# Loads of queries, keys and values cut into pieces of some 1.3 KB with gaps between them in DRAM, for all but the first four units

## The chip, the cores and the metric

The kernel runs on one core of a Trainium2 chip. The metric is the device time of one execution in microseconds (us). TensorE is PE in the rows, its weight loads PEld; VectorE is DVE, ScalarE ACT, GpSimd POOL, and SyncE is SP. SP issues the loads, ACT the stores. All of them go through the same 16 DMA engines of the core. The rows call the queue of SP's transfers q1, that of ACT's q10, and those that bring instructions q8 and q14.

## What is computed

Attention for 8 batches and 8 heads with 32 global and 512 local positions (head size 64): a global position looks at all positions, a local one at the 32 global ones and at the local ones at most 32 away. On its output `x` (8 x 576 x 512) a gated layer follows:

```
s_g = scale * q_g @ k_all^T                 out_g = softmax(s_g) @ v_all
s_l = concat(scale * q_l @ k_g^T, where(|i-j| <= 32, scale * q_l @ k_l^T, -1e9))
out_l = softmax(s_l) @ concat(v_g, v_l)
x = heads side by side (8 x 576 x 512)
gate = sigmoid(sum over k of conv_w[k] * x[position - 4 + k])       (5 taps)
result = (gate * (x @ w_val)) @ w_out
```

## The kernel before

The host lays the inputs out anew (`_layout`, ahead of the launch and outside the time). Two heads of one batch make a unit, so there are 32 units (`NU`), four to a batch. For each unit there is one array of queries and keys, 128 partitions x 1248 floats (`qk`, 4992 bytes a row), and one of values, 128 x 1950 floats (`vw`, 7800 bytes a row: 15 windows x 2 heads x 65).

Each unit is loaded by two transfers, `load_qk(u)` and `load_v(u)`, which go through `transfer` (`nc.sync.dma_start`) into one of 4 buffers for each kind. A row of the array is one contiguous stretch in DRAM and one in the partition it goes to. The weights come in 8 more transfers; those of `w_val` are cut into four stretches of 1 KB a partition, those of `w_out` come as rows of 4 KB. Thirteen loads are issued first of all (`FIRST`: the mask, q/k and v of units 0 to 3, the four parts of `w_val`); every later load has a place in one long line that is written out by hand (`ORDER`: `iq5` issues the q/k load of unit 5, `iv5` its v load, `wi4` the load of a weight). `transfer` ties a later load to the last PE instruction ahead of it in that line, so that a load is issued when PE has come that far.

The same line fixes the order of all work on each engine. For unit u: `s` are 128 small score matmuls on q/k (`l_s`, L522), `mx` and `exp` the softmax on DVE and ACT, `t` the transposes (L555, or L263 in halves of 64 rows), `av` 128 small matmuls on v (`l_av`, L574), `eps`/`norm` the division, `xt` a transpose (L601), `conv` the taps of the gate on DVE. For batch b: `gs`, `gav` are the scores and the weighted sums of the global positions (L425 and L477, the latter needs v of all four units), `g1`/`g2` the large matmuls of the gated layer (L706, L734), `ob` the copy of a result into one of 3 buffers and `st` its store of 256 KB, issued by ACT. From about 280 us on no unit is left and PE runs g1 and g2 almost alone.

Of the kernel before, what the change touches and what calls it, by code (L numbers as in the profile page):

```python
# [19 lines left out]
B, H, SL, SG, D = 8, 8, 512, 32, 64  # L20
DM = H * D
KW = 5
P = 128
NDT = DM // P
NU = B * NDT
NC32 = SL // 32
NPOS = 21
NWIN = 14
SCALE = 0.125
NEG = -1.0e30  # L30
QC = SL + 2 * SG
QK = QC + NPOS * 32


def chunk_pos(c):
    return c + c // 3


def win_pos(w):
    return w + w // 3  # L40


def block_win(m):
    return min(max(m - 1, 0), NWIN - 1)


def pos_chunk(p):
    return -1 if p % 4 == 3 else p - p // 4
# [113 lines left out]
FIRST = "q0 m0 q1 w0 q2 v0 q3 w1 v1 w2 v2 w3 v3"  # L162
# [78 lines left out]
def attention_moe(ctx, tc, qk, vw, maskd, w_val, w_out, out):  # L241
# [27 lines left out]
    small = cp.tile([P, 2 * P + NDT * KW * 2], I32, name="small")  # L269
    mask = small[:, :2 * P].bitcast(mybir.dt.bfloat16).rearrange("p (i c) -> p i c", i=4)  # L270
# [75 lines left out]
    def transfer(out, in_):  # L346


        ins = nc.sync.dma_start(out, in_).ins
        if last_pe:  # L350
            tc.add_manual_dep(ins, last_pe[0].name, after, reason="a load's place in the line")
# [43 lines left out]

    loads = {}

    def load_qk(u):
        t = sb.tile([P, QK], F32, tag="qk", name=f"qk{u}", bufs=RINGS["qk"])
        transfer(t, qk[u])  # L400
        loads.setdefault(u, [None, None])[0] = t

    def load_v(u):
        t = sb.tile([P, NWIN + 1, 2, E1], F32, tag="v", name=f"v{u}", bufs=RINGS["v"])
        transfer(t, vw[u])
        loads.setdefault(u, [None, None])[1] = t


# [3 lines left out]
    def g_s(b):  # L412
        units = [loads[u][0] for u in range(NDT * b, NDT * b + NDT)]
        s = [pair(f"gs{b}.{h}").rearrange("p a c -> p (a c)")[:, P:P + 544] for h in range(2)]
        for part in range(2):
            for n in range(8):
# [5 lines left out]
                else:  # L422
                    keys = qkt[rows, QC + 512:QK]
                cols = slice(0, 384) if part == 0 else slice(384, 544)
# [398 lines left out]
    for u in range(NU):  # L823
        if ("qk", u) not in first:
            plan.add(f"iq{u}", "SP", lambda u=u: load_qk(u), [f"iq{u - 1}"] if ("qk", u - 1) not in first else [],
                     take=[("qk", u)])
            plan.add(f"lq{u}", "DMA", lambda: None, [f"iq{u}"])
        if ("v", u) not in first:
            plan.add(f"iv{u}", "SP", lambda u=u: load_v(u), [f"iq{u}"] if ("qk", u) not in first else [],
                     take=[("v", u)])  # L830
            plan.add(f"lv{u}", "DMA", lambda: None, [f"iv{u}"])

    for b in range(B):
# [3 lines left out]
        for h in range(2):  # L837
            n = f"{b}.{h}"
# [111 lines left out]
    with tc.manual_schedule():  # L950
        for kind_, n in first:
            if kind_ == "qk":
                load_qk(n)
            elif kind_ == "v":
                load_v(n)
            elif kind_ == "w":
                wraws[n]()
            else:
                nc.sync.dma_start(small, maskd.bitcast(I32))
        V.memset(zf, 0.0)  # L960
        V.memset(zero, 0.0)
        V.tensor_copy(zr, zf)
        make_identity(nc, ident)
        G.tensor_scalar(out=nident, in0=ident, scalar1=-1.0, scalar2=None, op0=ALU.mult)
        G.memset(xgT[:, :, :, :KW - 1], 0.0)
        A.activation(out=table, in_=zf[:, :1], func=AF.Exp)
        keep_clock(2, 7, zf)
        last_pe.clear()
        held = None
        for t in plan.order():  # L970
            n = len(G.seen)
            t.emit()
            if t.lock and t.eng == "DVE":
                held = V.seen[-1]
            if t.lock and t.eng == "POOL" and held is not None:
                tc.add_manual_dep(G.seen[n], held.name, after, reason="a GpSimd step's place among VectorE's")
# [6 lines left out]
def _layout(np, q_l, k_l, v_l, q_g, k_g, v_g, moe_w_val, moe_conv_w, moe_w_out):  # L983
    def pair_t(a):
        return a.transpose(0, 1, 3, 2).reshape(NU, P, a.shape[2])

    qk = np.zeros((NU, P, QK), q_l.dtype)
    qk[:, :, :SL] = pair_t(q_l)
    qg = pair_t(q_g)
    qk[:, :D, SL:SL + SG] = qg[:, :D]  # L990
    qk[:, D:, SL + SG:QC] = qg[:, D:]
    kl = pair_t(k_l).reshape(NU, P, NC32, 32)
    kg = pair_t(k_g)
    vl = v_l.reshape(NU, 2, NC32, 32, D)
    vg = v_g.reshape(NU, 2, SG, D)
    vp = np.empty((NU, NPOS, 32, 2, D), v_l.dtype)
    for p in range(NPOS):
        c = pos_chunk(p)
        qk[:, :, QC + 32 * p:QC + 32 * p + 32] = kg if c < 0 else kl[:, :, c]
        vp[:, p] = (vg if c < 0 else vl[:, :, c]).transpose(0, 2, 1, 3)  # L1000
    vw = np.ones((NU, P, NWIN + 1, 2, D + 1), v_l.dtype)
    for w in range(NWIN):
        vw[:, :, w, :, :D] = vp[:, win_pos(w):win_pos(w) + 4].reshape(NU, P, 2, D)
    vw[:, :, NWIN, :, :D] = vp[:, [chunk_pos(c) for c in (9, 10, 11, 12)]].reshape(NU, P, 2, D)
    mask = np.zeros((P, 4, P), np.float32)
    r = np.arange(32)
    for m in range(NC32):
        i, j = divmod(m, 4)
        for a in range(4):
            c = pos_chunk(win_pos(block_win(m)) + a)  # L1010
            if c >= 0:
                far = np.abs((32 * m + r)[:, None] - (32 * c + r)[None, :]) > 32
                mask[32 * j:32 * j + 32, i, 32 * a:32 * a + 32][far] = NEG
    convT = moe_conv_w.T.reshape(NDT, P, KW).transpose(1, 0, 2).reshape(P, NDT * KW)
    raw = {"w_val": moe_w_val, "convT": convT, "w_out": moe_w_out}
    raw = {n: np.ascontiguousarray(a).view(np.int64) for n, a in raw.items()}
    small = [mask.astype(ml_dtypes.bfloat16).reshape(P, 4 * P).view(np.int64), raw.pop("convT")]
    return {"qk": qk, "vw": vw, "mask": np.concatenate(small, 1), **raw}


# [22 lines left out]
```

## Time and profile before

| | us |
|---|---|
| three runs: lowest, median, highest | 373.08, 376.45, 379.93 |
| the profiled execution | 372.64 |
| its span, first to last instruction | 370.8 |
| busy in it: PE, DVE, ACT | 342.6, 312.3, 224.5 |
| granted clock of PE, mean | 0.994 |

The profiled execution lies at the lower end of the three runs. A busy PE need not be PE at its peak, since matmuls are pipelined. "issue" in a row is time in which an engine waited for nothing that the profile shows.

### The profile page before, as it was taken

What the parts mean: (1) busy time and instruction counts of PE and PEld (TensorE: products, weight loads), DVE (VectorE), ACT (ScalarE), POOL (GpSimd) and SP (SyncE); (2) the same over time, 40 slices, a digit from 0 to 9 for tenths busy, and PEclk for the clock granted to TensorE, in tenths of its full rate; (3) what the DMA queues carried; (4) which work ended last, traced back from release to release, by engine and by line L of the source; (5) the groups of instructions that cost most, each with busy time, mean ns of one, the idle gap of its engine ahead of it and who ended that gap; (6) DMA issues with size and microseconds to landing.
All of it is one profiled execution on the core that took longest, in us unless ns stands there. A gap on an engine that the chain in (4) does not pass through costs nothing.

```text
span 370.8 us, 15157 instructions
## 1 busy us (share of the span) xinstructions
PE 342.6 (92%) x6560; PEld 273.8 (74%) x6560; DVE 312.3 (84%) x1034; ACT 224.5 (61%) x580; POOL 12.3 (3%) x23
## 2 busy tenths in 40 slices
PE   6698888999979998997989999999899999999994
PEld 3556567777867777776768877888778888888893
DVE  4999789998869988997879799999676999999751
ACT  3779688797848786866384857755386524232111
POOL 1340000000000000000000000000000000000000
PEclk9999999999999999998999999999999999999999
DMA  8987496787557184841627625904661000120304
GB/s 271 409 344 264 143 320 252 217 328 277 167 179 284 45 332 173 283 154 69 216 84 299 255 86 188 358 31 170 209 259 57 5 0 0 58 83 2 144 28 141
DMA packets 17106, 66.62 MB, mean 180 GB/s; under 512 B 1808, under 2 KB 3984, under 8 KB 17040
## 3 DMA queue, kind: packets, MB, share of 16 engines
q1 hardware_dynamic: 12240, 57.01, 42.8%
q10 hardware_dynamic: 4800, 8.65, 6.3%
q8 instruction: 51, 0.84, 0.9%
q14 instruction: 15, 0.12, 0.1%
HBM read 56.74 MB, written 8.91 MB: 177 GB/s over the span
## 4 chain that ended last, share of the span: by engine, by line
PE 79%; DMA 9%; DVE 6%; issue 4%; ACT 1%; DVEq 0%; SPq 0%
PE psum L734 25%; PE psum L706 23%; PE psum L574 8%; PE psum L522 7%; PE psum L263 4%; DMA v<-in_vw_dram 4%; PE psum L477 3%; PE psum L601 3%; DMA out_dram<-ob 3%; PE psum L555 2%; DVE pm L233 2%; DMA qk<-in_qk_dram 2%; PE psum L678 1%; PE psum L425 1%; DVE gate L233 1%
## 5 line engine op out<-in xcount | busy, mean ns | idle before, releaser
L541 ACT ACTIVATE pm<-pm,mx 128x128 f32<-128x128 f32 x256 | 80.0, 394 | 19.2 <-DVE mx L233 19.2
L233 DVE SCALAR_TENSOR_TENSOR gate<-xc,cw,gate 128x512 f32<-128x512 f32 x120 | 87.5, 748 | 1.7 <-ACT gate L324 0.6
L233 DVE CUSTOM_DVE_ANT_0 pm<-psum,small 128x128 f32<-128x128 f32 x256 | 57.4, 286 | 7.3 <-PE psum L522 7.1
L706 PE MATMUL psum<-xh,wvh 128*128 128x512 f32 x128 | 52.5, 410 | 0.8 <-issue 0.6
L734 PE MATMUL psum<-woh,gh 128*128 128x512 f32 x128 | 52.6, 411 | 0.0
L706 PE MATMUL psum<-xl,wvh 128*128 128x512 f32 x128 | 50.2, 392 | 0.0
L706 PE MATMUL psum<-xh,wvl 128*128 128x512 f32 x128 | 50.2, 392 | 0.0
L734 PE MATMUL psum<-wol,gh 128*128 128x512 f32 x128 | 50.0, 390 | 0.2 <-issue 0.2
L734 PE MATMUL psum<-woh,gl 128*128 128x512 f32 x128 | 50.1, 392 | 0.0
L574 PE MATMUL psum<-v,pts 128*32 128x65 f32 x2048 | 36.7, 223 | 7.6 <-issue 5.5
L522 PE MATMUL psum<-qk 64*32 64x128 f32 x2048 | 36.6, 273 | 5.8 <-DMA qk<-in_qk_dram 2.4
L574 PEld LDWEIGHTS psum<-v,pts 128*32 128x32 f32 x2048 | 32.1, 111 | 12.7 <-issue 8.2
L331 ACT COPY pts<-psum 128x512 f32<-128x512 f32 x53 | 30.0, 588 | 14.6 <-PE psum L263 8.0
L522 PEld LDWEIGHTS psum<-qk 64*32 64x32 f32 x2048 | 29.1, 105 | 12.0 <-issue 5.1
L690 ACT ACTIVATE gate<-gate 128x512 f32<-128x512 f32 x32 | 19.5, 627 | 16.9 <-DVE gate L233 16.8
L706 PEld LDWEIGHTS psum<-xh,wvh 128*128 128x128 f32 x128 | 24.4, 190 | 6.5 <-issue 0.7
L734 PEld LDWEIGHTS psum<-woh,gl 128*128 128x128 f32 x128 | 24.0, 188 | 5.7 <-issue 0.4
L233 DVE SCALAR_TENSOR_TENSOR gv<-gate,psum 128x512 f32<-128x512 f32 x32 | 21.8, 684 | 7.6 <-PE psum L706 7.4
L734 PEld LDWEIGHTS psum<-woh,gh 128*128 128x128 f32 x128 | 24.2, 189 | 5.3 <-issue 0.5
L706 PEld LDWEIGHTS psum<-xh,wvl 128*128 128x128 f32 x128 | 24.2, 189 | 5.3
L706 PEld LDWEIGHTS psum<-xl,wvh 128*128 128x128 f32 x128 | 24.2, 189 | 5.0 <-issue 0.8
L734 PEld LDWEIGHTS psum<-wol,gh 128*128 128x128 f32 x128 | 24.1, 189 | 4.1
(124 smaller groups left out, 529.9 us busy)
## 6 DMA issues: line engine op xcount, KB each, us to landing
v<-in_vw_dram SPq DMA_DIRECT2D x32, 975.0 KB, 6.8
qk<-in_qk_dram SPq DMA_DIRECT2D x32, 624.0 KB, 5.9
out_dram<-ob ACTq DMA_DIRECT2D x32, 256.0 KB, 2.3
wraw<-in_w_val_dram SPq DMA_DIRECT2D x4, 512.0 KB, 12.1
wraw<-in_w_out_dram SPq DMA_DIRECT2D x4, 512.0 KB, 3.5
out_dram<-obg SPq DMA_DIRECT2D x4, 64.0 KB, 2.0
out_dram<-obg ACTq DMA_DIRECT2D x4, 64.0 KB, 2.2
small<-in_mask_dram SPq DMA_DIRECT2D x1, 148.0 KB, 3.9
```

Of the source, the lines that this page charges most:

```text
L233: ins = made(*args, **kwargs)
L263: on_pe(T.matmul(out, in_, ident[D * r:D * r + D, D * r:D * r + D], is_transpose=True, **more))
L331: A.copy(out, in_)
L477: on_pe(T.matmul(ag[SG * c:SG * c + SG, :], pgt[:k, s, SG * c:SG * c + SG], vt[:k, w, h, :], start=(n == 0), stop=(n == len(steps) - 1)))
L522: on_pe(T.matmul((sx, sy)[h][32 * j:32 * j + 32, i, :], qkt[rows, 32 * m:32 * m + 32], qkt[rows, k0:k0 + P], start=True, stop=True))
L541: A.activation(out=pm[:, h, i, :], in_=pm[:, h, i, :], func=AF.Exp, bias=mx[:, c:c + 1], scale=-1.0)
L555: on_pe(T.transpose(pt[:, i, :], pm[:, h, i, :], ident))
L574: on_pe(T.matmul(ax[32 * j:32 * j + 32, h, E1 * i:E1 * i + E1], q, vt[:, block_win(4 * i + j), h, :], start=True, stop=True))
L601: on_pe(T.matmul(xt[:, P * i:P * i + P], xs[:, i].rearrange("p h d -> p (h d)"), ident, start=(i == 0 or u not in XP), stop=(u not in XP), ...
L690: A.activation(out=g, in_=g, func=AF.Tanh, scale=0.5)
L706: on_pe(T.matmul(box["pv", e], w[:, e, t * P:t * P + P], x, start=(t == 0 and q == 0), stop=(t == NDT - 1 and q == 2)))
L734: on_pe(T.matmul(box["po", r], g[:, e, rs], w[:, e, :], start=(e == 0 and q == 0), stop=(e == NDT - 1 and q == 2)))
```

## The change

In DRAM a row of `qk` is now 4 pieces of 312 floats (1248 bytes) at a distance of 320 floats, a row of `vw` 6 pieces of 325 floats (1300 bytes) at a distance of 336 floats. The gaps hold zeros and are not read. For every load after `FIRST` the transfer reads the pieces without the gaps and writes them side by side into the partition as before. For the four units in `FIRST` the host puts a row's floats side by side at the row's start and all the padding at its end; their transfers read one stretch a row as before, at a row distance of 5120 bytes (q/k) and 8064 bytes (v) in place of 4992 and 7800.

```diff
+PIECES = {"q": 4, "v": 6}
+LINE_PAD = 16
...
+    def row(t, src, u, kind, size):
+
+        n = PIECES[kind]
+        if f"{kind}{u}" in FIRST.split():
+            transfer(t, src[u].rearrange("p n c -> p (n c)")[:, :size])
+        else:
+            transfer(t.rearrange("p (n c) -> p n c", n=n), src[u, :, :, :size // n])
+
     def load_qk(u):
         t = sb.tile([P, QK], F32, tag="qk", name=f"qk{u}", bufs=RINGS["qk"])
-        transfer(t, qk[u])
+        row(t, qk, u, "q", QK)
...
-        transfer(t, vw[u])
+        row(t.rearrange("p w h c -> p (w h c)"), vw, u, "v", VW)
...
+    def pieces(a, kind):
+        n = PIECES[kind]
+        c = a.reshape(NU, P, -1).shape[2] // n
+        to = np.zeros((NU, P, n, c + (-c % LINE_PAD or LINE_PAD)), a.dtype)
```

No instruction changes its place on any engine; on SP the later loads change their shape. These are SP's rows from the last load of `FIRST` on (`wraw` is a weight, the number behind a tile's name its buffer), before the change:

```order
L349 DMA v_108<-in_vw_dram 128x1950
L349 DMA qk_366<-in_qk_dram 128x1248
L349 DMA wraw_526<-in_w_out_dram 128x1024
L349 DMA qk_564<-in_qk_dram 128x1248
L349 DMA qk_566<-in_qk_dram 128x1248
L349 DMA qk_632<-in_qk_dram 128x1248
L349 DMA wraw_790<-in_w_out_dram 128x1024
L349 DMA v_822<-in_vw_dram 128x1950
```

And these are the same rows of SP after it:

```order
L352 DMA v_108<-in_vw_dram 128x1950
L352 DMA qk_366<-in_qk_dram 128x4x312
L352 DMA wraw_526<-in_w_out_dram 128x1024
L352 DMA qk_564<-in_qk_dram 128x4x312
L352 DMA qk_566<-in_qk_dram 128x4x312
L352 DMA qk_632<-in_qk_dram 128x4x312
L352 DMA wraw_790<-in_w_out_dram 128x1024
L352 DMA v_822<-in_vw_dram 128x6x325
```

The order stands; each q/k load is now 128 x 4 stretches and each v load 128 x 6, in place of 128.

## Rows read from the trace of the kernel before

**Rows 1.** Page, part 1: busy us and share of each engine.
```profile
PE 342.6 (92%) x6560; PEld 273.8 (74%) x6560; DVE 312.3 (84%) x1034; ACT 224.5 (61%) x580; POOL 12.3 (3%) x23
```

**Rows 2.** Page, part 4: shares of the chain that ended last, by engine.
```profile
PE 79%; DMA 9%; DVE 6%; issue 4%; ACT 1%; DVEq 0%; SPq 0%
```

**Rows 3.** The chain in order of time: start us, us, what.
```profile
29.25 6.05 DMA qk<-in_qk_dram
...
36.75 1.58 issue
...
52.07 8.42 DMA v<-in_vw_dram
...
99.12 9.59 DMA out_dram<-ob
...
187.16 1.80 issue
```

**Rows 4.** PE's waits: tile, line, releaser, us in total, times, longest us.
```profile
PE psum L574 <- issue: 5.5, 5, 1.8
PE psum L477 <- issue: 3.8, 3, 2.0
PE psum L522 <- DMA qk<-in_qk_dram: 2.4, 2, 1.7
PE psum L574 <- DVE ob L233: 1.8, 1, 1.8
...
PE psum L522 <- issue: 1.5, 2, 1.3
...
PE psum L477 <- DMA v<-in_vw_dram: 1.2, 1, 1.2
```

**Rows 5.** Stretches: length, PE, PEld, DVE, ACT, POOL busy (xcount), clock, DMA share, GB/s.
```profile
36.80:49.30 12.50, 10.77 (x255) 7.51 (x254) 9.98 (x47) 9.42 (x26) 0.17 (x1) 1.00 0.57 192
49.30:82.90 33.60, 30.76 (x765) 24.57 (x766) 30.64 (x112) 27.71 (x72) 2.44 (x4) 1.00 0.79 272
```

**Rows 6.** Page, part 3: queue, packets, MB, share of 16 DMA engines.
```profile
q1 hardware_dynamic: 12240, 57.01, 42.8%
q10 hardware_dynamic: 4800, 8.65, 6.3%
q8 instruction: 51, 0.84, 0.9%
```

**Rows 7.** Stretches as in rows 5, two before a stop, one without.
```profile
79.20:81.60 2.40, 2.40 (x67) 2.06 (x66) 2.18 (x6) 2.40 (x6) 0.62 (x1) 1.00 0.85 354
136.80:139.00 2.20, 2.20 (x36) 1.66 (x39) 2.17 (x12) 1.21 (x3) 0.00 (x0) 1.00 1.00 414
...
290.40:291.50 1.10, 1.10 (x86) 1.10 (x80) 1.10 (x2) 0.46 (x1) 0.00 (x0) 1.00 0.05 15
```

**Rows 8.** DMA queues in 180.4 to 181.6 us, only a v load running.
```profile
q1 hardware_dynamic: 66, 0.51, 101.4%
```

**Rows 9.** DMA queues in 12 to 20 us, first loads with 1 KB stretches among them.
```profile
q1 hardware_dynamic: 1400, 3.22, 102.8%
```

**Rows 10.** DMA queues in 100.1 to 102.9 us, after the store issued at 99.12.
```profile
q1 hardware_dynamic: 133, 0.94, 100.7%
```

**Rows 11.** DMA queues in 254.6 to 256.0 us, a q/k load and a store together.
```profile
q1 hardware_dynamic: 83, 0.40, 69.5%
q10 hardware_dynamic: 82, 0.17, 30.8%
```

**Rows 12.** DMA queues in 14.90 to 18.06 us, among the first loads.
```profile
q1 hardware_dynamic: 498, 1.25, 100.0%
q8 instruction: 1, 0.02, 1.9%
```

**Rows 13.** DVE's wait for a store's landing, 98 to 111 us.
```profile
DVE ob L233 <- DMA out_dram<-ob: 2.8, 1, 2.8
```

**Rows 14.** DVE and the others in one stretch, columns as in rows 5.
```profile
110.00:160.00 50.00, 48.40 (x1020) 38.58 (x1012) 45.96 (x164) 39.19 (x104) 0.00 (x0) 1.00 0.59 210
```

**Rows 15.** SP's issues in order of time: start us, us, instruction.
```profile
7.81 4.04 SPq L349 DMA_DIRECT2D v<-in_vw_dram  x1
```

**Rows 16.** DMA queues in 0 to 12.87 us.
```profile
q1 hardware_dynamic: 1329, 4.00, 85.6%
```

More of the change, by code (lines that the diff above doesn't have):

```diff
@@ L32 @@
 QK = QC + NPOS * 32
+VW = (NWIN + 1) * 2 * (D + 1)
+PIECES = {"q": 4, "v": 6}
+LINE_PAD = 16
 def chunk_pos(c):
@@ L1017, in _layout @@
     small = [mask.astype(ml_dtypes.bfloat16).reshape(P, 4 * P).view(np.int64), raw.pop("convT")]
-    return {"qk": qk, "vw": vw, "mask": np.concatenate(small, 1), **raw}
+    def pieces(a, kind):
+        n = PIECES[kind]
+        c = a.reshape(NU, P, -1).shape[2] // n
+        to = np.zeros((NU, P, n, c + (-c % LINE_PAD or LINE_PAD)), a.dtype)
+        for u in range(NU):
+            if f"{kind}{u}" in FIRST.split():
+                to[u].reshape(P, -1)[:, :n * c] = a[u].reshape(P, -1)
+            else:
+                to[u, :, :, :c] = a[u].reshape(P, n, c)
+        return to
+    return {"qk": pieces(qk, "q"), "vw": pieces(vw, "v"), "mask": np.concatenate(small, 1), **raw}
 def kernel(**inputs):
```

## Prediction

> **What bounds the kernel now.** I read the shares of the engines first, then the chain that ended last, then PE's waits, and then the DMA queues in short stretches. PE is busy 342.6 of 370.8 us [rows 1] and holds 79% of the chain [rows 2]; DVE has 312.3 us. The remaining 28 us of PE are what a change to the loads can touch. Three things stand in them.
>
> First, "issue": 4% of the chain, some 14 us [rows 2]. The reader is to see that most of it is few and long: 5.5, 3.8 and 1.5 us in 10 stops of PE [rows 4], two of them 1.58 us at 36.75 and 1.80 us at 187.16 [rows 3]. They come at fixed places in PE's instructions: between the stop at 36.75 and that at 49.26 lie 255 + 254 = 509 of them, from there to the stop at 82.84 765 + 766 = 1531 [rows 5], which with a few unlisted semaphore waits is 2 x 256 and 6 x 256. Queue q8 carried 0.84 MB in 51 packets [rows 6]: PE's 13,120 instructions divided by 51 are 257 a packet. So PE stops where one packet of instructions ends and the next has not come. Before two of the stops the DMA engines were 0.85 and 1.00 busy; where PE ran 86 matmuls in 1.10 us with 0.05 on the DMA engines, it went on [rows 7]. I read this as instruction packets that stand behind load packets. That they do is inferred from place and time; no row names the releaser.
>
> Second, loads: PE waits 2.4 us for q/k and 1.2 us for v [rows 4], and the chain runs through loads that took 6.05 us (unit 5's q/k) and 8.42 us (unit 7's v) [rows 3]. Third, a store: issued at 99.12, it landed 9.59 us later [rows 3]; DVE waited 2.8 us for its buffer [rows 13] and PE 1.8 us behind DVE [rows 4].
>
> **What the change costs.** A packet of 7.8 KB takes 1.014 x 16 x 1.2 us / 66 = 295 ns [rows 8]. In 12 to 20 us the mean packet has 3.22 MB / 1400 = 2.30 KB and takes 1.028 x 16 x 8 us / 1400 = 94 ns [rows 9]. A line through both is 36.5 ns a KB and 10 ns a packet. So a 1300-byte piece takes 57.5 ns and a v row 345 in place of 295; a 1248-byte piece takes 55.6 ns and a q/k row 222 in place of 192. Each engine carries 8 rows of a load, so a v load grows by 0.40 us and a q/k load by 0.24. Over 28 units that is 18 us on each engine; q1 goes from 42.8% [rows 6] to 47.6% of the span, hidden where a load is early. The page DMA: Bandwidth & Descriptors of the Trainium skill (Why small descriptors are slow) speaks against cutting: a packet costs a fixed 3 cycles or so beside its 32-byte beats. By it a 1300-byte piece would lose 3 in 44, 7%, a v load 0.17 us; the 10 ns of the rows are the larger loss.
>
> Where a load is just in time PE pays: unit 5's q/k 0.24 us, unit 4's v 0.4, unit 7's v, behind unit 5's v and unit 8's q/k, 0.40 + 0.24 + 0.40 = 1.0, and I add 0.5 for loads that are now barely early: 2.2 us, between 0 (if the freed waits let PE come no earlier to them) and 4. The first four units read the same stretches at another row distance; I price that at nothing, since the first loads run at 102.8% of 16 engines already [rows 9] and the bytes are the same.
>
> **What it gives.** (a) Queues share an engine packet by packet: from 254.6 to 256.0 us q1 and q10 moved 83 and 82 packets, though one has twice the bytes [rows 11]. So a store's eight packets, once they alternate with loads, stand behind eight pieces of 57 ns in place of eight rows of 295: 1.9 us sooner. Of PE's 1.8 us behind the store I take 1.5. The same page (Queues, rings and completion order) says that an engine drains a whole packet of some 9 to 17 descriptors from one queue before it turns to the next. The equal counts of rows 11 do not show that; by it a waiting packet would stand behind 9 x 295 = 2.7 us now and 9 to 17 pieces, 0.5 to 1.0 us, then, and the gain in (b) would come all the same.
>
> (b) What already lies ahead in an engine must go first. After the store of 99.12 the engines moved 133 packets in 2.8 us before its own began, 8 each [rows 10]. If that is a number of packets, an instruction packet meets 8 x 57 = 0.5 us in place of 2.4. If it is a number of bytes, it meets the same 60 KB, 17% slower. The trace doesn't decide: in 14.90 to 18.06 us an instruction packet came at the end of 3.16 us in which 498 / 16 = 31 packets passed each engine, of 2.5 KB in the mean, 78 KB together [rows 12]. If it was asked for at the start of that, bytes count; when it was asked for no row says. I take packets, because a stop of 1 to 2 us goes away with 2 us and still mostly with 1, and price 9 of the 10.8 us of stops; the ends are all of the chain's 14 us, and a loss of 0.4 us at each of seven stops, 3 us.
>
> Sum on PE: -9 - 1.5 + 2.2 = -8.3 us. Not all reaches the end, because DVE must come sooner too: from 110 to 160 us it is busy 45.96 of 50 us [rows 14]. I take three quarters, -6.2. From the profiled 372.64 us that gives 366.4. The median of the runs is 376.45, 3.8 us above that execution; a new median will hold some of it, so I predict half of it on top: **368 us**.
>
> **Rivals.** *The wait is one of bytes* (27%): for it speak rows 12, against it only that a queue of packets is the simpler picture. The stops stay or grow: +3 - 1.5 + 2.2 = +3.7 on PE, +2.8 at the end: 375 to 379 us. *PE gains and DVE takes it back* (12%): DVE's 4 us of idle in 50 speak for it, its own 2.8 us behind a store and ACT's waits for PE against: 371 to 375. *SP's issue blocks, and ACT's stores behind it* (10%, the slower side): a v load's issue took 4.04 us on SP [rows 15] when, by the order of `FIRST`, 204 packets and end marks an engine had been issued up to 12.87 us and 1329 / 16 = 83 were done [rows 16], so some 120 to 130 open. A cut v load alone puts 49 into each engine, a q/k load 33; unit 15's q/k with the v loads of 13 and 15, issued within 3 us ahead of the store at 99.12, make 131. Should ACT's issue stand behind SP's, ACT holds its exps for 2 to 4 us there and at one or two such places: +6 to +10 with PE behind ACT, 380 to 386. It decides from about 120 open packets on with a store behind them; with fewer nothing blocks.
>
> **How the numbers follow.** The forecast, that instruction packets and stores pass between pieces, has 51%. About 2% is what a measurement of this kernel can tell from no change: below 369 or above 384 us, from 376.45. The forecast's own range is 361 to 373, some two thirds of it below 369: 0.34, and 0.02 from the others, for faster. Slower takes the blocked issue and the worst of the byte case: 0.11. The rest, 0.53, is within 2%. The range: 360, where all stops and the store's wait go and loads cost nothing (372.6 - 14 - 1.5 and DVE's share back), to 379, the upper end of the byte case.
>
> **What would show it.** SP's queue with some 40,900 packets (12,240 and 28 x 128 x 8 more) and 47 to 48%. Right: PE's waits for "issue" on L574, L477 and L522 fall from 10.8 us to under 3, the chain's issue share to 1 or 2%, the slowest store lands in under 7 us, PE's waits for loads grow by 1 to 3 us. Wrong: stops of 1 to 2 us at the same places in PE's instructions under full DMA (bytes count); ACT's DMA issues of over 1 us (blocking); a v load that takes over 3 us on the engines alone (pieces cost more than 57 ns); or PE's new waits for DVE as large as the stops that went.

## The result: 1.2% slower, and the stops of PE stay

The changed kernel takes 378.9 us in the median against 373.6 us for the kernel before on the same chip; the ratio is 1.0123 with a 95% interval of 1.0079 to 1.0167. The forecast of 368 us and its sign were wrong. The medians here are of 20 runs each; the prediction had three runs of the kernel before. Executions of one and the same kernel spread by 3% and more here, and the ratios in this text leave out the runs far above the fastest of their kernel, so that a ratio and a quotient of two medians need not agree.

The profiled execution took 377.46 us, its span is 375.7 us. The page of the changed kernel, parts 1 to 4:

```profile
PE 346.5 (92%) x6560; PEld 277.1 (74%) x6560; DVE 312.2 (83%) x1034; ACT 224.4 (60%) x580; POOL 12.0 (3%) x23
...
PEclk9899999999999999998969999999999999999998
...
q1 hardware_dynamic: 40912, 57.01, 45.3%
q10 hardware_dynamic: 4800, 8.65, 6.4%
q8 instruction: 51, 0.84, 0.9%
...
PE 83%; DMA 7%; issue 5%; ACT 2%; DVE 1%; SPq 0%; DVEq 0%; ACTq 0%
```

The same bytes go in 3.3 times as many packets as in [rows 6], and "issue" has 5% of the chain where it had 4% [rows 2]. PE's waits (tile, line, releaser, us in total, times, longest; the lines have moved by 11, so L574 of before is L585, L477 is L488, L522 is L533, L734 is L745, and L233 is L236):

```profile
PE psum L585 <- issue: 7.6, 5, 3.5
PE psum L488 <- issue: 4.1, 2, 2.3
PE psum L533 <- DVE mx L236: 2.4, 1, 2.4
PE psum L488 <- DMA v<-in_vw_dram: 2.0, 2, 1.5
PE psum L533 <- DMA qk<-in_qk_dram: 1.8, 1, 1.8
...
PE psum L533 <- issue: 1.0, 1, 1.0
...
PE psum L745 <- issue: 0.7, 1, 0.7
```

Against [rows 4]: the waits for "issue" on the three lines are 12.7 us, not under 3, and were 10.8. The waits for loads are 3.8 us, as before (3.6 in [rows 4], and 0.2 for v on L574). PE's wait for DVE's `ob` (1.8 us) is gone. The stop on L745 is one near 281 us that comes back below. Four pieces of the chain in order of time (start us, us, what):

```profile
111.95 8.66 DMA v<-in_vw_dram
...
142.84 3.44 PE psum L745 x15
...
186.23 3.46 issue
190.53 5.79 PE psum L745 x15
```

The stop at 186 us was 1.80 us [rows 3]. Behind it 15 large matmuls take 5.79 us; the same number takes 3.44 us at 142.84, and 3.46 us in the kernel before at the place of the stop. When PE's instructions of the two traces are laid side by side, one by one, the changed kernel runs up to 2.5 us ahead or 1.7 us behind until 186 us, where it is 0.9 us ahead. Then it loses 1.7 us at that stop, 2.6 us in the large matmuls behind it, and 1.3 us at a stop near 215 us which before does not have. At the end it is 4.8 us late.

### The profile page after: what moved, and what is told of

Read it like the earlier page. It is cut to its first block, busy times and chain, and to the rows that moved or that the text cites. A ratio compares the mean times of both kernels' runs of the same rounds, so it can differ in the third digit from the quotient of the medians.

```text
span 375.7 us, 15157 instructions
## 1 busy us (share of the span) xinstructions
PE 346.5 (92%) x6560; PEld 277.1 (74%) x6560; DVE 312.2 (83%) x1034; ACT 224.4 (60%) x580; POOL 12.0 (3%) x23
## 3 DMA queue, kind: packets, MB, share of 16 engines
q1 hardware_dynamic: 40912, 57.01, 45.3%
## 4 chain that ended last, share of the span: by engine, by line
PE 83%; DMA 7%; issue 5%; ACT 2%; DVE 1%; SPq 0%; DVEq 0%; ACTq 0%
PE psum L745 26%; PE psum L717 23%; PE psum L585 8%; PE psum L533 8%; PE psum L266 4%; PE psum L566 4%; PE psum L612 3%; PE psum L488 3%; DMA wraw<-in_w_out_dram 3%; DMA v<-in_vw_dram 2%; DMA qk<-in_qk_dram 2%; PE psum L436 2%; PE psum L689 2%; ACT pm L552 1%; PE psum L510 0%
## 5 line engine op out<-in xcount | busy, mean ns | idle before, releaser
L236 DVE SCALAR_TENSOR_TENSOR gate<-xc,cw,gate 128x512 f32<-128x512 f32 x120 | 87.3, 747 | 1.6 <-ACT gate L327 0.4
L236 DVE CUSTOM_DVE_ANT_0 pm<-psum,small 128x128 f32<-128x128 f32 x256 | 57.4, 286 | 8.4 <-PE psum L533 8.2
L745 PE MATMUL psum<-woh,gh 128*128 128x512 f32 x128 | 53.6, 419 | 0.0
L745 PE MATMUL psum<-wol,gh 128*128 128x512 f32 x128 | 50.9, 398 | 0.7 <-issue 0.7
L745 PE MATMUL psum<-woh,gl 128*128 128x512 f32 x128 | 51.1, 399 | 0.0
L585 PE MATMUL psum<-v,pts 128*32 128x65 f32 x2048 | 36.6, 222 | 7.7 <-issue 7.6
L533 PE MATMUL psum<-qk 64*32 64x128 f32 x2048 | 37.0, 277 | 5.2 <-DVE mx L236 2.4
L585 PEld LDWEIGHTS psum<-v,pts 128*32 128x32 f32 x2048 | 31.7, 110 | 12.7 <-issue 11.0
L533 PEld LDWEIGHTS psum<-qk 64*32 64x32 f32 x2048 | 29.6, 107 | 10.6 <-issue 3.0
L745 PEld LDWEIGHTS psum<-woh,gl 128*128 128x128 f32 x128 | 24.6, 192 | 6.4 <-issue 0.9
L745 PEld LDWEIGHTS psum<-woh,gh 128*128 128x128 f32 x128 | 24.9, 194 | 5.6 <-issue 0.6
L236 DVE SCALAR_TENSOR_TENSOR gv<-gate,psum 128x512 f32<-128x512 f32 x32 | 21.7, 682 | 7.6 <-PE psum L717 7.4
L745 PEld LDWEIGHTS psum<-wol,gh 128*128 128x128 f32 x128 | 24.7, 193 | 4.3
## 6 DMA issues: line engine op xcount, KB each, us to landing
out_dram<-ob ACTq DMA_DIRECT2D x32, 256.0 KB, 2.4
```

The source lines that it names most:

```text
L236: ins = made(*args, **kwargs)
L533: on_pe(T.matmul((sx, sy)[h][32 * j:32 * j + 32, i, :], qkt[rows, 32 * m:32 * m + 32], qkt[rows, k0:k0 + P], start=True, stop=True))
L585: on_pe(T.matmul(ax[32 * j:32 * j + 32, h, E1 * i:E1 * i + E1], q, vt[:, block_win(4 * i + j), h, :], start=True, stop=True))
L745: on_pe(T.matmul(box["po", r], g[:, e, rs], w[:, e, :], start=(e == 0 and q == 0), stop=(e == NDT - 1 and q == 2)))
```

## What an instruction packet waits for

The prediction's step (b) can be tested at one place. Counted in PE's instructions, the stops on instruction packets lie whole multiples of 256 apart in both kernels. In quiet stretches the packet for the next 256 starts about 1.1 us after PE has begun the instruction 309 ahead of the packet's first; call that the moment it is asked for. This is fitted to the starts, no row names a request. Besides, no two of these packets start less than 3.2 us apart in any trace. The packet that is short near 139 us was asked for at 136.8 us before, and at 135.76 us in the changed kernel. What queue q1 moved from then until the packet started, in the kernel before (136.8 to 139.0 us):

```profile
q1 hardware_dynamic: 174, 0.89, 97.5%
q8 instruction: 1, 0.02, 2.7%
```

and in the changed kernel (135.76 to 138.06 us):

```profile
q1 hardware_dynamic: 711, 0.87, 106.1%
q8 instruction: 1, 0.02, 3.1%
```

The wait is 2.2 and 2.3 us, the bytes ahead are 0.89 and 0.87 MB, 55 KB an engine, and the packets are 174 and 711. It is not the number of packets that counts, and bytes fit. Single waits scatter. Counted from the request, or from 3.45 us behind the start of the packet before where that is later, the packets that met load data (from 25 us on) waited 0.4 to 5.9 us before (median of 18: 2.6) and 1.0 to 4.6 us after (median of 20: 2.3). Some 11 packets an engine went ahead of them before and 41 after, with 59 and 52 KB.

## Experiments

The ratio of each kernel is taken against runs of the kernel before beside it on the same chip. A condition shown for the load (`row`) stands in the layout of the arrays as well. "Stop" means the gap between two neighbouring instructions of PE at the places 256 apart.

**1. Row distance alone.** The arrays get the distance between rows that the change gives them, but each row stays whole.

```
-        if f"{kind}{u}" in FIRST.split():
+        if True:            # every load: one stretch a row, rows further apart
```

> Every row of q/k and v lies in one stretch at the padded row distance (5120 and 8064 bytes), for all units; nothing is cut. Theory A (the pieces cost: 18 us more of transfer on each engine, so instruction packets and loads come later): no change from before, ratio 0.995 to 1.005, q1 back to 12,240 packets and about 43%. Rival B (the row distance in DRAM costs): the whole 1.2% of the change stays, ratio about 1.012.

Ratio 0.9942 (0.9878 to 1.0006), 375.0 us against 374.7. No cost of the distance can be measured.

**2. Only v in pieces.**

```
-        if f"{kind}{u}" in FIRST.split():
+        if kind == "q" or f"{kind}{u}" in FIRST.split():
```

> Only v rows are cut in 6 pieces, q/k rows lie whole at the padded distance. Theory A: v carries 28 x 0.40 of the 17.9 us of added transfer, so some two thirds of the loss, ratio 1.005 to 1.010; PE's stops on instructions as long as with the whole change. Rival B: 1.012 again. Rival C (SP's longer issue of 0.54 us in place of 0.33 is what costs): half, 1.006.

Ratio 0.9963 (0.9918 to 1.0009). 28 loads that each last 0.3 to 0.4 us longer on the engines cost nothing that can be measured, so the price of a load on the engines does not by itself reach the end.

**3. Smaller pieces.** q/k in 8, v in 13.

```
-PIECES = {"q": 4, "v": 6}
+PIECES = {"q": 8, "v": 13}
```

> q/k rows in 8 pieces of 624 bytes, v rows in 13 of 600. By 10 ns a packet and 36.5 ns a KB a v row takes 415 ns and a q/k row 262: 43 us more of transfer on each engine than whole rows, 2.4 times the change's 18. Theory A with a wait counted in bytes: instruction packets under load wait 2.5 us or more, PE's stops 14 to 20 us, ratio 1.02 to 1.04. If the wait is counted in packets but deeper than 50 of them: waits fall below 2 us and the stops below 10 us, ratio 1.00 to 1.02.

Ratio 1.0387 (1.0315 to 1.0458), 387.3 us. The median wait of an instruction packet, counted as above, is 2.4 us although 80 packets an engine go ahead of it: again not a matter of their number. Pieces of some 0.62 KB from 211.48 to 214.59 us, where a train of six loads runs:

```profile
q1 hardware_dynamic: 1582, 0.98, 114.0%
```

That is 1.14 x 16 x 3.11 us / 1582 = 35.9 ns a piece. The 3.11 us are also the wait of one instruction packet, from its request to its start, behind 61 KB an engine; so the wait is no fixed 2.2 us either.

**4. No loads.** The kernel before without the q/k and v loads of units 4 to 31, which then work on the data of units 0 to 3; the result is another one, the work on all engines is the same.

```
     def load_qk(u):
+        if u >= 4:
+            loads.setdefault(u, [None, None])[0] = loads[u % 4][0]
+            return
```

> The kernel before without the q/k and v loads of units 4 to 31: each of them computes on the tiles of units 0 to 3, so the outputs after the first batch are other numbers. It prices all that these loads do to the rest. Theory A: the 10 stops of PE on instructions (10.8 us) and its waits for loads and the store (5 us) go but for 1 or 2 us, 360 to 366 us by the executions, ratio 0.965 to 0.985. If the stops are of another cause (PE's instructions come too slowly by themselves): the stops stay near 10 us, ratio above 0.985.

358.04 us, ratio 0.961 (0.9558 to 0.9663), and the four runs lie within 0.5%. PE's waits for "issue" in it (the last column is the longest one):

```profile
PE psum L580 <- issue: 2.7, 3, 1.3
...
PE psum L528 <- issue: 1.2, 1, 1.2
```

The stops of the first 190 us, up to 2.2 us each before, are gone or below 1 us. All stops together are 5.7 us in place of 15.8, which is 10.1 of the 14.6 us between the two spans (356.2 and 370.8). That loads make these stops was inferred in the prediction; it is now shown. It does not hold for every stop that the prediction counted: that near 260 us stands here at its length. PE's wait without these loads, from 240 to 250 us:

```profile
PE psum L580 <- issue: 1.3, 1, 1.3
```

and in the kernel before, from 255 to 265 us:

```profile
PE psum L574 <- issue: 1.3, 1, 1.3
```

The spread between runs seems to go with the loads too, as far as four runs tell.

**5. Only q/k in pieces.**

```
-        if f"{kind}{u}" in FIRST.split():
+        if kind == "v" or f"{kind}{u}" in FIRST.split():
```

> Only q/k rows are cut in 4 pieces, v rows lie whole at the padded distance. With v alone cut the time was 0.9963 of before and with none cut 0.9942, so if the parts add up, the q/k pieces carry the loss: ratio 1.007 to 1.015. In the trace: the burst of four q/k loads at about 200 us ends later, and PE stops again on instructions near 212 us for 1 us or more (it stopped 0.8 us there before). If the loss needs both cuts (longer transfers that meet an instruction packet only together): ratio 0.993 to 1.003.

Ratio 1.009 (1.0034 to 1.0147). The q/k loads, the smaller ones with the smaller price, seem to carry most of the loss, which no term of the prediction foresaw. The stop near 212 us that was expected did not come: it is 0.18 us.

**6 and 7. Two loads moved, after and before.** v20 is issued earlier and v22 later, so that both are not open together near 186 us.

```
- ... mx20.1 gav4.1 tap15:ACT ... g1.2.3.3 iv20 ... conv14.2 iv22 st.1.3 ... s23@56 gt5.0T@3 iv21
+ ... mx20.1 gav4.1 iv20 tap15:ACT ... g1.2.3.3 ... conv14.2 st.1.3 ... s23@56 gt5.0T@3 iv22 iv21
```

> The changed kernel with two loads moved in the line: unit 20's v some 5 us earlier, unit 22's v some 14 us later, so that no v load runs while PE's instruction packets near 181 and 186 us are asked for. Theory (loads hold up instruction packets, the long stop lets PE's clock fall): the stop of 3.5 us at 186 us shrinks below 1 us, no half clock after it, some 4 us less than the changed kernel, ratio to before 0.998 to 1.006. If the stop is not those loads' doing: it stays, 1.01 to 1.015.

> The same two moves in the kernel before. Theory: its stop of 1.8 us at 187 us shrinks to 0.7 us or less, ratio 0.993 to 0.998. If the stop is not those loads' doing: ratio 1.000, the stop stays at 1.5 us or more.

Moved in the changed kernel: 1.0097 (1.0022 to 1.0173), no gain. Moved in the kernel before: 0.9941 (0.9889 to 0.9994), just below 1. In both the stop at 186 us shrinks to 1.15 and 1.17 us, and in both a stop grows near 211 us, to 2.9 and 2.1 us, because v22 now lengthens the loads there. Here loads that were moved away from one instruction packet met another.

**8. The changed kernel, second trace.**

> A second profile of the changed kernel. If the loss is made at the places that the first profile shows, the stop of over 2.5 us near 186 us with half clock behind it, and one of 1 us near 214 us, are there again. If the long stops fall elsewhere each time, the loss is one of chance: more time under load for each packet, no fixed place.

379.33 us. The stop at 186 us is 3.42 us again and that at 212 us is 1.38; a third one, near 230 us, is new:

```profile
PE psum L533 <- issue: 4.0, 1, 4.0
```

**9 and 10. q/k in pieces in one half of the units.** Units 4 to 15, then units 16 to 31; v whole.

```
-        if kind == "v" or f"{kind}{u}" in FIRST.split():
+        if kind == "v" or u > 15 or f"{kind}{u}" in FIRST.split():
```

> Only the q/k rows of units 4 to 15 are cut in four pieces; q/k of units 16 to 31 and all v rows are whole. With all q/k rows cut the ratio was 1.009 (1.0034 to 1.0147), with no row cut 0.994. Theory early: the loss comes from the first 100 us, where the load queue is busy almost without a gap and q5 and v12 are used within 0.1 us of their landing, so that 0.24 us more for each load is waited for. Then this kernel carries all of it: ratio 1.006 to 1.012, PE's waits for qk or v loads 1 to 2 us above those of before, and no stop behind 180 us other than before has. Theory late (the burst of q24 to q27, which lasts longer and meets the fetch of PE's instructions at 212 us, and the stop at 186 us): ratio 0.992 to 0.999, the stop at 212 us below 0.3 us. Theory spread: the loss falls on both halves, 0.999 to 1.004 here and in the kernel with units 16 to 31.

> Only the q/k rows of units 16 to 31 are cut in four pieces; q/k of units 4 to 15 and all v rows are whole. Theory early: nothing, ratio 0.992 to 0.998. Theory late: all the loss of the kernel with every q/k row cut, ratio 1.004 to 1.012; the burst q24 to q27 lasts over 1.5 us longer than before and the stop at 212 us is over 1 us. Theory spread: 0.999 to 1.004.

0.9976 (0.9926 to 1.0026) for the early units, 1.0037 (0.9997 to 1.0076) for the late ones. The early loads, which are the just-in-time ones of the prediction, cost nothing that can be measured. Whether the late ones carry all of the 0.9% is not decided by these intervals. The stop near 211 us stayed at 0.08 us in the late kernel, so the late theory missed there.

**11. v in pieces and v20, v22 moved.** The two edits that had read below 1, together.

> A version meant to beat both: v rows cut in six pieces, q/k rows whole, and the load of v20 issued one step earlier, right behind the last gather-matmuls of batch 4, v22 later, as in the version of before with these two loads moved. If what was measured apart (0.9963 for v alone, 0.9941 for the move) adds up: ratio 0.988 to 0.992. If both only scatter round before's time: 0.995 to 1.002. Stop at 186 us 1.0 to 1.3 us in place of 2.0, and a stop of about 2 us at 212 us.

Ratio 1.0006 (0.9958 to 1.0055). The stop at 186 us is 0.92 us, that near 211 us 2.62. What looked like two gains of half a per cent did not add up to one. Only the move alone (7) read below 1 with its whole interval, and it was not timed again.

**12. The kernel before, second trace.**

> The kernel before once more, for a second trace of it. If the longer stops of the changed kernel at 186 us (3.4 to 3.7 us in two traces) and at 212 us (1.3 to 1.4 us) are its own, they read 2.0 and 0 to 0.2 us here again, and the sum of PE's stops is 14 to 17 us. If they are chance, one of them reads over 1 us longer here. The stop of 4.2 us near 233 us, which some traces have and some have not, may stand here as well; then the sum is about 20 us.

378.45 us, 6 us above the first trace of the same kernel. The stop near 233 us that the second trace of the changed kernel had (8) stands in it:

```profile
PE psum L522 <- issue: 4.2, 1, 4.2
```

So this stop is no property of the change. The stop at 186 us is 2.62 us, that near 211 us 0.34.

**13 and 14. Eight loads.** v20 to v23 and q24 to q27 whole in the changed kernel, then these eight alone in pieces.

```
+BURST = "v20 v21 v22 v23 q24 q25 q26 q27".split()
-        if f"{kind}{u}" in FIRST.split():
+        if f"{kind}{u}" in FIRST.split() + BURST:      # 13: these whole
+        if f"{kind}{u}" not in BURST:                  # 14: only these in pieces
```

> The changed kernel with the rows of eight loads whole again: v20 to v23 and q24 to q27. Theory burst (six loads behind each other each last longer when cut, 0.4 us for a v and 0.24 us for a q/k load, so the train v21, v23, q24 to q27 ends 1.8 us later and meets an instruction packet that it missed before): the stop behind the train goes from 1.3 us to at most 0.4, that at v20 and v22 from 3.5 us to 2.0 to 2.7, and the ratio from 1.012 to 1.002 to 1.007. Theory spread (all cut loads take their share): ratio 1.008 to 1.014.

> The kernel before with these eight loads cut and no other. Theory burst: the train of six lasts 15 us and more from the first issue to the last landing, in place of 13.2 to 14.2, the stop behind it is 1.0 to 1.5 us, and the ratio is 1.004 to 1.010. Theory spread: 8 of the 56 cut loads bring a seventh of 1.2%, ratio 0.998 to 1.003.

With the eight whole the median of six runs is 378.5 us against 374.15 of before, no better than the changed kernel; in its trace the stop behind the train of loads is 0.04 us, that near 186 us 2.87 us, and the one near 233 us is there with 4.17 us. With the eight alone in pieces the ratio is 1.0043 (0.997 to 1.0116), which fits either theory. The stops are clear where the times are not. PE's waits of the kernel with only these eight in pieces, from 184 to 192 us:

```profile
PE psum L586 <- issue: 3.2, 1, 3.2
```

and from 212 to 220 us:

```profile
PE psum L586 <- issue: 1.1, 1, 1.1
```

Both stops of the changed kernel stand in it at their length, 3.42 and 1.32 us.

**15 and 16. Third traces of both kernels.**

> The changed kernel once more for a third trace. If the two longer stops belong to the change: 3.3 to 3.8 us at v20 and v22, 1.2 to 1.5 us behind the train. If they were chance in two traces, at least one of them reads within 0.4 us of 2.0 and 0.

> The kernel before once more for a third trace. If the shorter stops belong to it: 2.0 to 2.7 us at v20 and v22, 0 to 0.4 us behind the train. The stop of 4.2 to 4.5 us near 233 us may come or not: it stood in one of two traces of either kernel.

The changed kernel took 384.04 us: 2.60 us at 186 us, 1.38 behind the train, 4.22 near 233 us. The kernel before took 369.41 us: 1.80, 0.22 and none. At 186 us both lie outside what was expected.

**17 and 18. The train whole and the changed kernel side by side.**

> The changed kernel with v20 to v23 and q24 to q27 whole, timed again beside the changed kernel itself. Theory burst: the stop behind the train at most 0.4 us, and the time 1.3 to 3 us below that of the changed kernel (ratio 1.004 to 1.009). Theory spread: the stop is gone, yet the time stays within 1 us of the changed kernel (ratio 1.009 to 1.014), since the loss is carried by other places.

> The changed kernel timed again: ratio 1.008 to 1.017, as measured first. The stop behind the train 1.2 to 1.5 us. If the stop of 4.2 us near 233 us belongs to kernels in which both kinds of rows are cut, it stands here and in the kernel with the train whole; if it is chance, in about one of the two.

Ratio 1.0073 (0.9999 to 1.0147) with the eight loads whole, 1.028 (1.0207 to 1.0354) for the changed kernel. The 1.028 is not to be leaned on: by the medians of all runs the changed kernel took 380.61 us (6 runs) beside 378.72 of before (17 runs), 0.5% more, and the kernel with eight loads whole 375.71 us (12 runs). Between these two the eight of the 56 cut loads make 4.9 us, which speaks for the burst theory, but is more than that theory gave (1.3 to 3 us); and the first timing of the same kernel (13) had not shown it. The stop behind the train is 0.09 and 1.41 us. The stop near 233 us is absent with the train whole and 4.49 us in the changed kernel.

## Where the time went

**The train of six loads, shown.** v21, v23, q24, q25, q26 and q27 are issued behind each other, tied to PE's place in the line. Each load ends with 16 landing marks, one an engine; the table has the first of q27's. From the first issue to the last landing before, 195.8 to 209.1 us, queue q1 did

```profile
q1 hardware_dynamic: 864, 4.55, 86.4%
```

and after, 199.1 to 214.6 us,

```profile
q1 hardware_dynamic: 3680, 4.55, 87.2%
```

which is 0.864 x 13.3 = 11.5 us on each engine before and 0.872 x 15.5 = 13.5 us after, 2.0 us more; by the prediction's prices it would be 2 x 0.40 + 4 x 0.24 = 1.8. Both the train and the instruction packet hang on PE's place, so the packet is asked for 12.66 us after v21's issue, in every trace whose order is unchanged:

| kernel | first landing of q27 after v21's issue, us | packet starts at, us | stop, us |
|---|---|---|---|
| before, three traces | 12.55, 13.03, 13.01 | 12.70, 13.01, 12.93 | 0.00, 0.34, 0.22 |
| changed, eight loads whole, two traces | 12.81, 12.88 | 12.72, 12.86 | 0.04, 0.09 |
| only q/k in pieces | 13.68 | 13.68 | 0.18 |
| only v in pieces | 13.64 | 13.44 | 0.45 |
| only these eight in pieces | 14.54 | 13.99 | 1.32 |
| changed, four traces | 14.48 to 14.64 | 14.04 to 14.26 | 1.30 to 1.41 |
| smaller pieces | 16.46 | 15.77 | 3.04 |

A packet that before is asked for as the train ends now meets its last 1.4 us. With one kind of row in pieces the train lasts 1 us longer and the packet's head start covers most of that; with both kinds it does not. So effects of v and of q/k need not add up. The stop is PE's wait in the changed kernel from 211 to 219 us:

```profile
PE psum L585 <- issue: 1.1, 1, 1.1
```

and with the smaller pieces, 212 to 222 us:

```profile
PE psum L585 <- issue: 2.8, 1, 2.8
```

In the kernel before no wait for "issue" stands on this line from 207 to 216 us.

**The stop at 186 us, partly.** It is 3.68, 3.42, 2.60 and 2.60 us in four traces of the changed kernel and 2.02, 2.62 and 1.80 in three of before: 0.9 us more in the mean, with the ranges just overlapping. Over all traces whose order is unchanged it is 2.60 to 3.68 us (mean 3.1) in the seven with v20 and v22 in pieces, and 1.80 to 2.87 us (mean 2.2) in the nine with them whole. So the cut very likely lengthens it; what sets a single stop within these ranges stays open.

**The stop near 233 us, open.** It is either absent or 3.9 to 4.5 us long: in three of four traces of the changed kernel, in one of three of before, and in four of the twelve traces of the other kernels with loads. That is too few to say that the change makes it likelier. Where it comes the packet starts some 6 us later than where it does not, though PE, DVE and ACT do the same to within 0.1 us. In the kernel without loads a packet at the same place came late too, with no packet at all on the DMA engines from 211 to 215 us, and PE stopped for 1.45 us. So it is not loads alone that make this packet late, and no run shows what does.

**Two more stops.** One near 168 us also comes or does not come: 2.5 us in all four traces of the changed kernel, 2.24 us and twice none in the three of before, and 1.7 to 2.8 us in all twelve of the other kernels with loads, with whole rows (1) too. What decides can be read off. A q/k load is issued 0.68 us ahead of the packet's request in every one of these 19 traces. In the two without the stop the packet before had started 3.3 and 3.6 us ahead of the request, so this one could start within 0.35 us, ahead of the load's data. In the other 17 the packet before had started only 1.8 to 3.0 us ahead, which is less than any two packets lie apart, and 26 to 40 KB an engine went first. With q/k in pieces at this place the packet before is late by itself (1.8 to 2.5 us ahead in ten traces, 2.1 to 3.6 in the nine others), and the stop is 2.5 us in the mean in place of 1.6. PE's wait in the changed kernel from 160 to 175 us:

```profile
PE psum L488 <- issue: 2.3, 1, 2.3
```

The other, near 281 us, is 1.04 to 1.45 us in the four traces of the changed kernel and 0.63 us and twice none in those of before: 0.9 us more. This is the wait on L745 above. With whole rows (1) it is absent as well, but with the smaller pieces (3) too, so that the change makes it is likely and not shown.

**The clock.** Stretches of the changed kernel (length, PE, PEld, DVE, ACT, POOL busy with counts, granted clock, DMA share, GB/s):

```profile
186.00:189.50 3.50, 0.23 (x15) 0.07 (x4) 3.18 (x6) 3.00 (x8) 0.00 (x0) 0.88 0.21 77
189.50:196.00 6.50, 6.31 (x20) 4.90 (x21) 1.40 (x3) 2.48 (x7) 0.00 (x0) 0.54 0.12 43
```

PE was busy 0.23 of 3.5 us; right behind that the granted clock reads 0.54, most of the stretch at 1.2 in place of 2.4 GHz, and 15 matmuls of L745 take 5.79 us (above) in place of 3.44. The stop's price is then 3.5 us and 2.4 more. It is no fixed rule in these traces: in the second trace of the changed kernel the stop of 3.42 us at the same place left the clock alone, and in the kernel before the clock fell behind a stop of only 2.24 us at 169 us, to 0.90 in the mean of this stretch:

```profile
169.40:187.30 17.90, 15.77 (x383) 12.93 (x383) 14.13 (x61) 9.75 (x27) 0.00 (x0) 0.90 0.41 143
```

**Sum.** All stops of over 0.25 us together are 15.8, 18.9 and 12.7 us in the three traces of before, mean 15.8, and 17.1, 22.7, 24.7 and 22.3 us in the four of the changed kernel, mean 21.7. The 5.9 us between them go with the 6.3 us between the mean times of the same traces (373.5 and 379.8 us), which is more than the 4.6 us that the ratio of 1.0123 gives. Of them 1.2 us behind the train are shown to come from the cut, and 0.9 us at 186 us and 0.9 us near 281 us are likely to. The stops near 168 and 233 us make 1.8 us each in these means; of the first some 0.9 us go with the pieces when all traces are taken, the second may be chance. The other places together are 0.7 us shorter after the change. So the cause of the loss is shown for a fifth of it, likely for somewhat under another half, and open for the rest. Why q/k in pieces alone cost 0.9% with hardly a stop behind its train is not settled: its one trace has stops of 16.9 us in all, and a wait of PE for DVE's `ob` of 2.5 us.

## The prediction, step by step

**What bounds the kernel** stood: "issue" is in the main the wait for instruction packets, and loads make most of it (4); the stop near 260 us, 1.3 of the 10.8 us, is not theirs.

**Price of a piece**: right for a piece, too high for the whole. From 211.84 to 213.22 us the changed kernel moved pieces of 1.22 KB at 1.059 x 16 x 1.38 us / 411 = 56.9 ns, from the row

```profile
q1 hardware_dynamic: 411, 0.50, 105.9%
```

against 55.6 predicted. Over the whole span q1 took 0.453 x 375.7 - 0.428 x 370.8 = 11.5 us more on each engine, not 18: the share is 45.3% and not 47.6. The median pieces measure 54 ns (q/k) and 56 ns (v), which makes 28 x 8 x (4 x 54 - 192 + 6 x 56 - 295) ns = 14.6 us; the other 3 us were not traced. The page DMA: Bandwidth & Descriptors of the Trainium skill (Why small descriptors are slow) names a fixed cost of some 3 cycles a packet beside 32-byte beats. By it a 1300-byte piece would take 7% over a sixth of a row of 295 ns, an estimate of 52.6 ns; the trace shows 56 ns, 14%, and decides.

**PE's waits for loads**, +2.2 us: wrong, 3.8 us against 3.8. The cut early q/k loads cost nothing that can be measured (9). The step added longer loads to a PE whose place in time it left as it was, while other waits moved: the stop near 49 us is 0.9 us shorter in the mean of the traces (0.9 us in place of 1.7). That the one paid for the other is argued and not shown.

**(a) The store**: right, and then mostly given back. It landed 6.8 us after its issue in place of 9.59 [rows 3]; the longest in the other traces is 6.8 to 7.2 us after and 8.7 and 8.9 before. PE's 1.8 us behind DVE [rows 4] went, and DVE's wait [rows 13] too. But PE came 2.5 us sooner to v12, whose load takes 8.66 us (the chain above) in place of 7.26. PE takes it up less than 0.1 us after its landing in either kernel, and now waits 1.5 us there. Most of what the store's buffer released, the next load held.

**(b) Instruction packets**: the step that failed. It took what lies ahead in an engine as a number of packets, 0.5 us of pieces. The runs show no such number: 11, 41 and 80 packets an engine went ahead with whole rows, pieces and smaller pieces, and the median wait was 2.6, 2.3 and 2.4 us, behind some 50 to 60 KB. The prediction had a row that said so, 78 KB ahead of one packet [rows 12], and set it aside because no row told when that packet was asked for. It could have been told from the trace: the starts of instruction packets that met no load give PE's place at the request, and with it the wait of most others. In place of -9 us the step brought nothing: the waits for "issue" on the three lines rose by 1.9 us in the first trace. The rule of the same page of the Trainium skill (Queues, rings and completion order), one queue drained for some 9 to 17 descriptors before the next, would have brought the gain as well; the equal waits speak against it, as [rows 11] did.

**Rivals.** *The wait is one of bytes* is what happened; its 375 to 379 us hold the profiled 377.46 and the median of 378.9. Its loss was put down evenly, 0.4 us at each stop, and to late loads. As far as the runs place it, it sits where a longer train of loads reaches a packet that it had just missed, and at a few stops that come in some traces and not in others. *DVE takes the gain back* had no gain to work on. *SP's issue blocks, and ACT's stores behind it*: half of it. Its count of 120 to 130 open packets is for 12.87 us, where the next v load's issue began, which took 2.89 us; at 7.81 us, where the one of 4.04 us began, the same count gives 162 less 52 done, 110. SP's issues became longer (line, instruction, ns lowest/median/highest, first and last start); before

```profile
L349 SPq DMA_DIRECT2D qk<-in_qk_dram x32: 327/328/1047, 0.7 to 252.6; - x32
```

and after

```profile
L352 SPq DMA_DIRECT2D qk<-in_qk_dram x32: 402/540/1519, 0.7 to 257.4; - x32
```

but ACT's did not wait behind them:

```profile
L931 ACTq DMA_DIRECT2D out_dram<-ob x32: 338/339/609, 99.5 to 368.8; - x32
```

**The chances.** 0.53 on "within 2%" was the share that came true, but by luck: it had been built around 368 us, and 378.9 lies in the range only by its upper end, which was the rival's. Starting from one profiled execution also misled: the three traces of the kernel before take 369.4 to 378.5 us, with 4 us of that in one stop that comes or does not come.

## What to carry to other kernels

Where PE runs on many short instructions, as here, its instruction packets queue behind load data, and the number of pieces does not matter: cutting rows doesn't let them through, it only makes the data ahead slower. Lay the times at which instruction packets are asked for beside the trains of loads, and look for a packet that is asked for just as a train ends: a few tenths of a us on each load of that train turn into a stop there, and a move of two loads only made another packet late. Trace a kernel several times before a stop of a few us is taken for its own.

## What the runs showed of the hardware that was not expected

- An instruction packet of 16 KB is asked for some 309 PE instructions ahead (fitted), starts no less than 3.2 us behind the one before, and at one place behind full queues waited 2.2 and 2.3 us with 174 and with 711 load packets ahead.
- All q/k and v loads of units 4 to 31 together cost this kernel 3.9%, two thirds of it through such waits, though PE waits under 4 us for late data.
- SP's issue of a load in pieces takes 0.54 us in the median, of a whole one 0.33.
- The spread of 3% between runs of one kernel was not seen without the loads: four runs lay within 0.5%.
- A stop of 3.42 us left PE's clock alone where one of 2.24 us was followed by half of it.
